# The last 64 rows: token weight, q tails and batch 1's k, v loaded in another shape and order, and the start planned anew

## The chip, the cores and the metric

The kernel runs on one core of one Trainium2 chip. The metric is the device time of one execution in microseconds. Three runs of the kernel before took 355.86, 356.5 and 356.73 us, median 356.5. One more execution was profiled; it took 356.91 us, and the span from its first to its last instruction is 355.1 us.

## The reference: what is computed

Linear attention, without a softmax, then an RMS norm per head, and a residual MLP that mixes tokens first and channels second. All inputs and the output are float32.

```python
kv  = einsum('bhsd,bhse->bhde', k, v)          # 8 batches, 8 heads, 576 rows, 64 channels
out = einsum('bhsd,bhde->bhse', q, kv)
x   = out / sqrt(mean(out*out, -1) + 1e-6) * g_norm      # heads side by side: [8, 576, 512]
tok = einsum('ts,bsd->btd', w_tok, alpha1*x + beta1)     # w_tok 576 x 576
u   = x + lam*tok
ch  = maximum((alpha2*u + beta2) @ w_ch1, 0) @ w_ch2     # 512 -> 2048 -> 512
y   = u + lam*ch
```

## The kernel before

**Tiling.** 576 rows are four chunks of 128 and a tail of 64. Chunk c of a tile holds every fourth row, since the loads give each partition four consecutive rows of 512 (`(p c) d`, c = 4); the last 64 rows, the tail, are loaded apart, on 64 partitions. Tails of an even and an odd batch share one tile of 128 partitions (`xtl`), so the MLP treats five chunks in odd batches and four in even ones. k and v have a second layout, "rows of nine" (`nine`): 64 partitions take nine consecutive rows each of one head, the other 64 partitions the same of its neighbour, 2304 bytes in one piece; the sum over rows in k'v does not care for their order.

**Stages of a batch.** k'v per head (`kv_product` on rows of nine, L695, or `kv_groups.main` and `tails` on rows of four, L798 and L808), split into two bf16 parts (`kvd`); q split likewise (`split_q`), turned (`qt_dma`: batch 1 on TensorE, L673, later batches by DMA transposes); the product q (k'v) and the norm (`qkv_groups`); the token product with the turned `w_tok` (`wt`) and the residual sum (`tok_groups`, `tok_first` for batch 0, L1242, sum at L1259); the turn of u (`ut_groups`; for batch 0 on TensorE, L1277); the channel MLP (`ch1_groups`, L1343 to L1370; `ch2_groups`, L1419). Batch 0 has its own fp32 code for the front: `kv_first`, `qt_first` (L730, and its tails L745) and `qkv_first` (L929, tails L954; the tail rows are scaled and rounded into `rtt` at L974 and L982).

**Constant work at the start.** `wt_groups` turns `w_tok`: its first 512 rows in L1565, its last 64 rows (`wst2`, 64 partitions of 576) by five TensorE transposes in L1588, and sums its columns in L1610 (`sums`, columns 0 to 511 and 512 to 575), which carries beta1 through the product. The staging tiles `wst`, `wst2` lie in `ht`, so that the MLP's first write of `ht` waits for their readers.

**What sets the order.** Every operation is noted with its engine, an assumed cost, what it reads and writes (keys). A list scheduler (`Prog.schedule`) then writes one static order per engine. Priorities follow from due times of the MLP's products (`mark`), and a table (`P.plan(due, 8, moves, on)`) adds to the priorities of single operations by their number, or fixes their engine. Until the first MLP product, where the scheduler sees nothing ready for TensorE, it writes filler products on a zeroed tile into the stream (`warm`, L1750); they stay in the stream whatever the real times are. The scheduler also assumes that TensorE's code comes in blocks of 256 instructions that take 5 to 6.6 us each (`fetched`, `fetch`).

**Loads.** All large loads go out on SyncE's queue in a fixed chain: for each half of batch 0's heads k, v, q and two q-tail loads (`load_first`, `load_q`, `load_first_tail`, L594); `w_tok` in two parts and its tail (L1521, L1525); then, behind a "gate" (the first four of nine products of batch 0's second half), batch 1's k and v (L608, with two tail loads each, L613) with `w_ch1`'s first quarter, q and the q tail between (L575), the other quarters (L1648), `lam`, and `w_ch2`'s quarters (L1659).

Of the kernel before, what the change touches and what calls it, by code (L numbers as in the profile page):

```python
# [19 lines left out]
TP = 640  # L20
# [443 lines left out]
def bass_transnormer_attn__then__resmlp_affine_kernel(  # L464
# [15 lines left out]
    with ExitStack() as stack:  # L480
# [38 lines left out]
        a2t = sb("a2t", [128, 4, TP + 16], BF16)  # L519
# [7 lines left out]
        wst2 = hst[0:64, 2304:2880]  # L527
# [39 lines left out]
        def load_main(tile, key, src, b, hs, eng="SP"):  # L567
# [4 lines left out]
                dma_us=3.7 if hs == ALL[0] else 1.5 if hs.start else 2.0)  # L572
# [11 lines left out]
        def load_first(a):  # L584
            for key, src, tile in (("kf", k, kf), ("vf", v, vf)):
                P.op("SP", 0.6, lambda e, src=src, tile=tile: e.dma_start(
                    nine(tile, 0, a).rearrange("p x c d -> p x (c d)"),
                    src[0, 4 * a:4 * a + 4].rearrange("(x y) (p c) d -> (y p) x (c d)",
                                                      y=2, c=9)),
                    w=[(key, a)], dma_us=2.0 if a and key == "vf" else 1.4)  # L590

        def load_first_tail(a):
            for y in range(2):
                P.op("SP", 0.45, lambda e, y=y: e.dma_start(  # L594
                    qft[0:64, 4 * a + 2 * y:4 * a + 2 * y + 2, :],
                    q[0, 4 * a + y:4 * a + y + 3:2, 512:576, :].rearrange("h s d -> s h d")),
                    w=[("qft0", a, y)], dma_us=0.2)

        def load_kv(b):
            j = (b + 1) % 2  # L600
            for tile, src, n in ((kf, k, "kf"), (vf, v, "vf")):
                if b > 1:
                    P.op("SP", 0.6, lambda e, src=src, tile=tile: e.dma_start(
                        tile[:, j].rearrange("p (z f) -> p z f", z=4),
                        src[b].rearrange("(z y) (p c) d -> (y p) z (c d)", y=2, c=9)),
                        w=[(n, j)], dma_us=3.1)
                    continue
                P.op("SP", 0.6, lambda e, tile=tile, src=src: e.dma_start(  # L608
                    rows512(tile).rearrange("p h c d -> p h (c d)"),
                    src[b, :, 0:512, :].rearrange("h (p c) d -> p h (c d)", c=4)),  # L610
                    r=["gate"], w=[(n, j)], dma_us=3.2)
                for g in range(2):
                    P.op("SP", 0.5, lambda e, tile=tile, src=src, g=g: e.dma_start(  # L613
                        rows64(tile)[64 * g:64 * g + 64],
                        src[b, 4 * g:4 * g + 4, 512:576, :].rearrange("h s d -> s h d")),
                        w=[(n + "t", g)], dma_us=0.2)

        def load_q(b, hs=ALL[0], tails=True):
            load_main(qf, "qf", q, b, hs)
            if tails:  # L620
# [8 lines left out]
        def split_q(b):  # L629
# [4 lines left out]
            for cs, hs in parts:  # L634
# [4 lines left out]
                if n == 1:  # L639
# [5 lines left out]
                kh, kl = ([qkeys(b, c, i, a) for c in cs for a in aa] for i in range(2))  # L645
# [7 lines left out]
        def qt_dma(b):  # L653
# [10 lines left out]
            for a, hs in enumerate(HALVES):  # L664
                for cs in PAIRS:
# [3 lines left out]
                    def f(e, cs=cs, t=t, hs=hs, n=n):  # L669
                        for h in range(4):  # L670
                            for i, c in enumerate(cs):
# [6 lines left out]
                                                           for x in keys_of(c, (a,))], w=[t])  # L678
                    P.op(act_dve(512 * n, 1.5), 0, lambda e, cs=cs, t=t, hs=hs, n=n: copy(
# [40 lines left out]
        def qt_first():  # L720
# [18 lines left out]
            def tail(a):  # L739
                t = P.ptile(1)  # L740

                def f(e):
                    for pr in range(2):
                        h = 4 * a + 2 * pr
# [36 lines left out]
        def kv_groups(b):  # L781
            if b > 1:
                yield from kv_nine(b)
                return
# [373 lines left out]
        def wtk(sc):  # L1158
            return [("wtm", sc)] if sc < 4 else [("wts", lo) for lo in (0, 512)]

        def tok_groups(b):
# [26 lines left out]
            def tails():  # L1188
                t = P.ptile(1)

                def f(e):
                    for sc in range(5):
                        for i in range(2):
                            w, r = tok_w(sc, 4), rsrc(i, sc)
                            if b >= MIX and sc == 4:
# [6 lines left out]
                                      for kk in wtk(s) + rkeys(i, s)], w=[t])  # L1202
# [313 lines left out]
        for i, hs in enumerate(HALVES):  # L1516
            load_first(i)
            load_q(0, hs, False)
            load_first_tail(i)
        for i in range(2):  # L1520
            P.op("SP", 0.6, lambda e, i=i: e.dma_start(  # L1521
# [271 lines left out]
```

## Time and profile before

| what | value |
|---|---|
| runs, median | 356.5 us |
| profiled execution, its own time | 356.91 us |
| its span | 355.1 us |
| TensorE busy | 344.1 us, 97% |
| VectorE, ScalarE, GpSimd busy | 238.7, 157.0, 22.2 us |
| DMA | 60.83 MB, mean 171 GB/s |
| granted TensorE clock | 1.00 throughout |
| first MLP product (L1343) | 31.09 us from the span's start |

How to read it: PE is TensorE's products, PEld its weight loads, DVE VectorE, ACT ScalarE, POOL GpSimd, SP SyncE, which issues loads and stores. A row of a timeline gives start, length, engine, line, operation, tiles, how many, and in brackets how long the engine idled before it and what ended that. A row of the chain of waits gives start, length and the work on the chain. A row of a window gives the busy time of each engine in that stretch, with the number of instructions.

### The profile page before, as it was taken

The numbers are of one execution on the slowest core, as the hardware profiler recorded it, in microseconds if no ns is written. First come the engines' busy times: TensorE is split into PE (matmuls) and PEld (weight loads), VectorE is DVE, ScalarE is ACT, GpSimd is POOL, SyncE is SP. The second block draws the span as 40 slices with busy tenths as digits, with TensorE's granted clock in tenths as the row PEclk, the third lists the DMA queues.
The fourth block names the chain that finished last, engine by engine and source line by source line (L and its number), as shares of the span: only waits on it lengthen the run. The fifth ranks groups of instructions, "written<-read, shape, count | busy, mean of one in ns | idle before, by whom it ended". The sixth has DMA issues, their size and how long they took to land.

```text
span 355.1 us, 7785 instructions
## 1 busy us (share of the span) xinstructions
PE 344.1 (97%) x3501; PEld 198.9 (56%) x3320; DVE 238.7 (67%) x365; ACT 157.0 (44%) x267; POOL 22.2 (6%) x30
## 2 busy tenths in 40 slices
PE   7998999999999999999999999999999999999996
PEld 6776644567554554467644654457744554457643
DVE  3679997874889579968883389945974378830021
ACT  3646961248722585038720386018620285007600
POOL 4161123300000000000000000000000000000000
PEclk9999999999999999999999999999999999999999
DMA  8999999999983599269704496244404010150022
GB/s 280 337 360 372 394 346 362 252 203 248 294 231 78 152 379 154 64 198 346 136 18 133 157 319 133 46 148 64 89 4 146 33 30 2 30 153 11 0 61 89
DMA packets 82761, 60.83 MB, mean 171 GB/s; under 512 B 55773, under 2 KB 66277, under 8 KB 82728
## 3 DMA queue, kind: packets, MB, share of 16 engines
q1 hardware_dynamic: 82704, 60.32, 58.7%
q8 instruction: 27, 0.44, 0.6%
q14 instruction: 6, 0.05, 0.0%
q10 hardware_dynamic: 24, 0.01, 0.0%
HBM read 38.82 MB, written 9.44 MB: 136 GB/s over the span
## 4 chain that ended last, share of the span: by engine, by line
PE 88%; DVE 6%; DMA 3%; issue 1%; SPq 0%
PE ps L1419 30%; PE ps L1370 18%; PE ps L1328 14%; PE ps L1168 7%; PE ps L695 4%; PE ps L1019 2%; PE ps L458 2%; PE ps L1197 1%; DMA vf<-in_v_dram 1%; DVE xm L1429 1%; DMA qt<-qs 1%; DVE a2b L1185 1%; DVE xm L1181 1%; PE ps L1400 1%; PE ps L1217 1%
## 5 line engine op out<-in xcount | busy, mean ns | idle before, releaser
L1419 PE MATMUL ps<-w,ht 128*128 128x512 bf16 x537 | 122.5, 379 | 2.3 <-issue 1.4
L1317 ACT ACTIVATE ht<-ps,hb 128x640 bf16<-128x640 f32 (+1 forms) x112 | 83.7, 747 | 48.7 <-PE ps L1370 35.9
L1419 PEld LDWEIGHTS ps<-w,ht 128*128 128x128 bf16 x560 | 53.5, 98 | 63.6 <-issue 2.0
L1370 PE MATMUL ps<-a2t,w 128*128 128x320 bf16 (+1 forms) x512 | 72.2, 299 | 0.4 <-DMA a2t<-a2b 0.4
L1370 PEld LDWEIGHTS ps<-a2t,w 128*128 128x128 bf16 x512 | 49.5, 98 | 21.4 <-DMA a2t<-a2b 0.8
L1328 PE MATMUL ps<-a2t,w 128*128 128x512 bf16 x232 | 52.7, 379 | 1.3 <-issue 0.6
L766 ACT ACTIVATE kvd<-ps 64x128 bf16<-64x128 f32 x24 | 6.5, 271 | 85.4 <-PE ps L695 85.3
L1328 PEld LDWEIGHTS ps<-a2t,w 128*128 128x128 bf16 x240 | 22.6, 98 | 26.5 <-DMA a2t<-a2b 0.4
L1429 DVE TENSOR_TENSOR xm<-ps,xm 128x512 f32<-128x512 f32 x31 | 20.7, 688 | 24.8 <-PE ps L1419 24.5
L1168 PE MATMUL ps<-rt,wt 128*128 128x512 bf16 x106 | 25.2, 379 | 0.4 <-issue 0.2
L1041 DVE TENSOR_REDUCE small<-sq 128x16 f32<-128x1024 f32 x14 | 16.8, 1214 | 12.9 <-ACT sq L1039 12.7
L1181 DVE TENSOR_TENSOR xm<-ps,xm 128x1024 f32<-128x1024 f32 x14 | 17.1, 1222 | 8.0 <-PE ps L1217 5.1
L695 PEld LDWEIGHTS ps<-vf,kf 64*64 64x64 f32 x1008 | 16.0, 135 | 6.3 <-issue 4.5
L564 ACT ACTIVATE qs<-qf 128x1024 bf16<-128x1024 f32 x13 | 13.4, 1049 | 13.5 <-DMA qf<-in_q_dram 10.7
L1185 DVE TENSOR_TENSOR a2b<-xm,a_bc 128x512 bf16<-128x512 f32 x28 | 18.7, 709 | 0.5
L771 DVE TENSOR_TENSOR kvd<-ps,kvd 64x128 bf16<-64x128 f32 x24 | 6.9, 288 | 18.0 <-ACT kvd L766 17.6
L695 PE MATMUL ps<-vf,kf 64*64 64x64 f32 x1008 | 17.9, 221 | 0.6 <-DMA vf<-in_v_dram 0.6
L1168 PEld LDWEIGHTS ps<-rt,wt 128*128 128x128 bf16 x112 | 10.9, 98 | 12.9 <-issue 0.4
L650 DVE TENSOR_TENSOR qs<-qf,qs 128x1024 bf16<-128x1024 f32 x14 | 16.9, 1217 | 1.5 <-ACT qs L564 1.5
L1060 DVE TENSOR_TENSOR xm<-ps,small 128x1024 f32<-128x1024 f32 x14 | 17.1, 1221 | 0.4
L1429 DVE TENSOR_TENSOR xtl<-ps,xtl 128x512 f32<-128x512 f32 x4 | 2.8, 692 | 20.2 <-PE ps L1419 20.1
L1019 PEld LDWEIGHTS ps<-kvd,qt 128*128 128x128 bf16 x224 | 13.9, 98 | 2.5 <-DMA qt<-qs 0.6
(146 smaller groups left out, 327.9 us busy)
## 6 DMA issues: line engine op xcount, KB each, us to landing
out_dram<-xm SPq DMA_DIRECT2D x31, 256.0 KB, 2.5
qf<-in_q_dram SPq DMA_DIRECT2D x7, 1024.0 KB, 11.4
kf<-in_k_dram SPq DMA_DIRECT2D x6, 1152.0 KB, 7.4
vf<-in_v_dram SPq DMA_DIRECT2D x6, 1152.0 KB, 8.5
stg<-in_moe_w_ch_dram SPq DMA_DIRECT2D x3, 1024.0 KB, 14.1
kf<-in_moe_w_ch_dram SPq DMA_DIRECT2D x2, 1024.0 KB
kf<-in_k_dram SPq DMA_DIRECT2D x2, 576.0 KB, 4.8
vf<-in_v_dram SPq DMA_DIRECT2D x2, 576.0 KB, 5.6
```

Of the source, the lines that this page charges most:

```text
L650: lambda e, hi=hi, lo=lo, src=src: e.tensor_tensor(out=lo, in0=src, in1=hi, op=ALU.subtract), r=kin + kh, w=kl, port=True)
L695: m = e.matmul(t.ap(slice(64 * x, 64 * x + 64))[:, y, 0:64], nine(kf, b, a)[r, x, c, :], nine(vf, b, a)[r, x, c, :], start=(c == 0), stop= ...
L1019: e.matmul(o, w, kvd[:, h, 0, :], start=True, stop=False)
L1060: P.op("DVE", dve_us(64 * m), lambda e: e.tensor_tensor(out=x3, in0=split(raw()), in1=inv, op=ALU.mult), r=[t, ("sm", sms)], w=xk, pri=-200)
L1168: m = e.matmul(t.ap()[:, i, :], tok_w(sc, c), rsrc(b, sc), start=(sc == 0), stop=(sc == 4))
L1181: P.op("DVE", dve_us(512 * n), lambda e: e.tensor_tensor(out=x, in0=t.ap(rows) if n > 1 else t.flat(rows), in1=x, op=ALU.add), r=[t] + xk, ...
L1185: P.op("DVE", dve_sb(512), lambda e, c=c: e.tensor_tensor(out=a2b[rows, c, :], in0=xv(b, (c,)), in1=a2_bc[rows, :], op=ALU.mult), r=xkeys( ...
L1317: o = P.op("ACT", act_us(n) + 0.07 * (b > 0), lambda e: e.activation(dst, src(), ACT.Relu, bias=hb[:, fj:fj + 1]) if b else e.activation(d ...
L1328: m = e.matmul(t.flat(), w, a2t[:, dj, 0:512], start=(dj == 0), stop=(dj == 3))
L1370: m = e.matmul(t.ap()[:, i, 0:n], w1[:, dj, 128 * fj:128 * fj + 128], a2t[:, dj, 320 * i:320 * i + n], start=(dj == 0), stop=(dj == 3))
L1419: m = e.matmul(t.flat(), ht[:, fj, 128 * c:128 * c + 128], w2[:, fj, :], start=(fj == 0), stop=(fj == 15))
L1429: P.op("DVE", dve_us(512), lambda e: e.tensor_tensor(out=x, in0=t.flat(), in1=x, op=ALU.add), r=[t] + keys, w=keys)
```

## The change

Six edits and a new table of moves.

1. The last 64 rows of `w_tok` go to 128 partitions: partition 2t + h holds half h of row t (256 values); the last 64 columns go to a small tile of their own, `wst3`. They are no longer turned by transposes, but by fp32 products with every second column of the identity, which pick out the rows of one half.
2. The turned tail gets keys of its own (`wtt`), so that products on token columns 0 to 511 no longer wait for it, nor for the second part of the column sums.
3. Batch 0's q tails are loaded by two transfers (even heads, odd heads) in place of four, behind `w_tok`'s first 512 rows; k, v, q of both halves move up.
4. Batch 1's k and v are loaded in rows of nine, two transfers in place of six, and go through `kv_nine`.
5. Batch 1's q tail goes to 128 partitions (heads 0 to 3 on the lower, 4 to 7 on the upper 64, four heads side by side), by two transfers; its split works on 128 x 256 values in place of 64 x 512, and one group of four transposes turns it, where there were two. It overwrites batch 0's q tail, whose readers it waits for.
6. `a2t` is wider by 48 columns, which nothing reads.
7. The table of moves has other entries: 69 operations with a changed priority where there were 46, and nine with a fixed engine where there were five. All operation numbers shift, so the entries do not compare one by one.

```diff
-        wst2 = hst[0:64, 2304:2880]
+        wst2, wst3 = hst[:, 2304:2560], hst[0:64, 2560:2624]
...
-        def load_first_tail(a):
-            for y in range(2):
-                P.op("SP", 0.45, lambda e, y=y: e.dma_start(
-                    qft[0:64, 4 * a + 2 * y:4 * a + 2 * y + 2, :],
-                    q[0, 4 * a + y:4 * a + y + 3:2, 512:576, :].rearrange("h s d -> s h d")),
-                    w=[("qft0", a, y)], dma_us=0.2)
+        def load_first_tail(y):
+            P.op("SP", 0.45, lambda e: e.dma_start(
+                qft[0:64, 4 * y:4 * y + 4, :], q[0, y:8:2, 512:576, :].rearrange("h s d -> s h d")),
+                w=[("qft0", a, y) for a in range(2)], dma_us=0.36)
...
         def load_kv(b):
             j = (b + 1) % 2
             for tile, src, n in ((kf, k, "kf"), (vf, v, "vf")):
-                if b > 1:
-                    P.op("SP", 0.6, lambda e, src=src, tile=tile: e.dma_start(
...
-                P.op("SP", 0.6, lambda e, tile=tile, src=src: e.dma_start(
-                    rows512(tile).rearrange("p h c d -> p h (c d)"),
-                    src[b, :, 0:512, :].rearrange("h (p c) d -> p h (c d)", c=4)),
-                    r=["gate"], w=[(n, j)], dma_us=3.2)
-                for g in range(2):
-                    P.op("SP", 0.5, lambda e, tile=tile, src=src, g=g: e.dma_start(
-                        rows64(tile)[64 * g:64 * g + 64],
-                        src[b, 4 * g:4 * g + 4, 512:576, :].rearrange("h s d -> s h d")),
-                        w=[(n + "t", g)], dma_us=0.2)
+                P.op("SP", 0.6, lambda e, src=src, tile=tile: e.dma_start(
+                    tile[:, j].rearrange("p (z f) -> p z f", z=4),
+                    src[b].rearrange("(z y) (p c) d -> (y p) z (c d)", y=2, c=9)),
+                    r=["gate"] if b == 1 else [], w=[(n, j)], dma_us=3.1)
 
         def load_q(b, hs=ALL[0], tails=True):
             load_main(qf, "qf", q, b, hs)
-            if tails:
+            if b == 1:
+                for g in range(2):
+                    P.op("SP", 0.6, lambda e, g=g: e.dma_start(
+                        qft[64 * g:64 * g + 64, 0:4, :],
+                        q[1, 4 * g:4 * g + 4, 512:576, :].rearrange("h s d -> s h d")),
+                        w=["qft1", "qft0"] + [("qft0", a, y) for a in range(2) for y in range(2)]
+                        if g == 0 else ["qft1g"], dma_us=0.35)
+            elif tails:
                 load_tail(qft, "qft%d" % (b % 2), q, b, 64 * (b % 2))
...
-                if n == 1:
+                if n == 1 and b == 1:
+                    src, hi, lo = qft[:, 0:4], qs[:, 4, 0:4, 0, :], qs[:, 4, 0:4, 1, :]
+                    kin, nh = ["qft1", "qft1g", "qft0"], 4
+                elif n == 1:
...
-                for cs in PAIRS:
+                for cs in PAIRS if a == 0 else PAIRS[:2]:
...
+                    if n == 1:
+                        P.op(act_dve(512, 1.5), 0, lambda e, t=t: copy(
+                            e, qt[:, :, 576:640].rearrange("p (g h) s -> p g h s", g=2),
+                            t.flat().bitcast(BF16)[:, 0:512].rearrange(
+                                "p (h g s) -> p g h s", h=4, g=2)),
+                            r=[t], w=[("qt", 4, x) for x in range(2)])
+                        continue
...
         def kv_groups(b):
-            if b > 1:
-                yield from kv_nine(b)
-                return
+            yield from kv_nine(b)
+            return
...
-        def wtk(sc):
-            return [("wtm", sc)] if sc < 4 else [("wts", lo) for lo in (0, 512)]
+        def wtk(sc, lo=0):
+            return [("wtt" if lo else "wtm", sc)] if sc < 4 else [("wts", lo)]
...
+        for what, i in (('k', 0), ('v', 0), ('q', 0), ('k', 1), ('v', 1), ('q', 1), ('w', 0), ('w', 1), ('t', 0), ('t', 1), ('w', 2)):
+            if what == "w":
+                load_wtok(i)
+            elif what == "q":
+                load_q(0, HALVES[i], False)
+            elif what == "t":
+                load_first_tail(i)
+            else:
+                load_first(i, what)
...
+                        for h in range(2 if sc < 4 else 1):
+                            r = slice(64 * h, 64 * h + 64)
+                            m = e.matmul(tail.flat(r)[:, 64 * sc:64 * sc + 64],
+                                         wst2[:, OFF[sc]:256:4] if sc < 4 else wst3,
+                                         ident[:, h:128:2] if sc < 4 else ident[r, r],
+                                         start=True, stop=True,
+                                         skip_group_check=True)
...
+        def load_wtok(i):
+            if i == 2:
+                P.op("SP", 0.6, lambda e: e.dma_start(
+                    wst2, moe_w_tok[512:576, 0:512].rearrange("t (h s) -> t h s", h=2)),
+                     w=["wst2"], dma_us=0.4)
+                P.op("SP", 0.6, lambda e: e.dma_start(wst3, moe_w_tok[512:576, 512:576]),
+                     w=["wst3"], dma_us=0.1)
```

More of the change, by code (lines that the diff above doesn't have):

```diff
@@ L644, in split_q @@
                     kin = [("qf", a) for a in aa]
-                kh, kl = ([qkeys(b, c, i, a) for c in cs for a in aa] for i in range(2))
+                kh, kl = ([qkeys(z, c, i, a) for c in cs for a in aa
+                           for z in ((0, 1) if c == 4 and b == 1 else (b,))] for i in range(2))
                 m = 64 * n * nh
@@ L1515, in bass_transnormer_attn__then__resmlp_affine_kernel @@
         P.chain = True
[L1516 to L1521, printed above, removed]
+        def load_wtok(i):
[5 more added lines that the diff above has]
+                     w=["wst3"], dma_us=0.1)
+                return
+            P.op("SP", 0.6, lambda e: e.dma_start(
                 wst[:, 2 * i:2 * i + 2, :],
@@ L1754, in bass_transnormer_attn__then__resmlp_affine_kernel @@
         P.plan(due, 8, {
[7 rows of a table removed]
-            154: "DVE", 181: "DVE", 182: "POOL", 211: "POOL", 215: "DVE"})
[10 rows of a table added]
+            59: "DVE", 67: "DVE", 88: "POOL", 148: "DVE", 177: "ACT", 180: "ACT", 182: "ACT",
+            184: "DVE", 204: "POOL"})
         P.synchronize()
```

39 lines of the change are left out of this document (15 added, 24 removed), and 17 rows, old and new, of the table start.

## The prediction

> **What bounds the kernel now.** I read the page first, from its top to the chain of waits.
>
> ```profile
> span 355.1 us, 7785 instructions
> PE 344.1 (97%) x3501; PEld 198.9 (56%) x3320; DVE 238.7 (67%) x365; ACT 157.0 (44%) x267; POOL 22.2 (6%) x30
> ...
> q8 instruction: 27, 0.44, 0.6%
> ```
>
> TensorE is busy 97% of the span, so a gain has to come out of TensorE time that computes nothing, or out of TensorE work itself. The next view is busy time by stretch: up to the first product of the channel MLP (31.09), up to the steady MLP (40.77), and on; the last columns are the granted clock, the busy share of the sixteen DMA engines, and GB/s.
>
> ```profile
> 5.89:31.09 25.20, 24.39 (x485) 19.35 (x490) 18.00 (x43) 14.85 (x38) 8.54 (x11) 1.00 1.06 350
> 31.09:40.77 9.68, 8.71 (x126) 6.40 (x96) 9.32 (x16) 7.11 (x10) 1.16 (x1) 1.00 1.03 394
> 40.77:60.00 19.23, 19.02 (x105) 8.50 (x107) 18.79 (x23) 10.29 (x20) 3.65 (x3) 1.00 1.04 371
> 66.00:81.00 15.00, 14.07 (x240) 9.12 (x224) 11.53 (x23) 5.40 (x12) 0.45 (x1) 1.00 0.95 181
> ```
>
> From 40.77 TensorE has no slack (19.02 of 19.23). From 31 to 60 VectorE is full too (28.11 of 28.91), and DMA throughout (1.06 to 1.03 to 1.04). The slack is before 40.77. I take it from the chain of waits, in order of time (start, length, what):
>
> ```profile
> 11.52 0.23 PE ps L954 x8
> ...
> 11.91 1.03 PE ps L1750 x4
> 12.94 1.21 PE ps L695 x72
> ...
> 15.31 0.33 PE ps L745 x2
> 15.65 0.54 PE ps L1750 x2
> ...
> 18.34 0.68 PE ps L1588 x5
> ...
> 23.63 0.25 PE ps L1610 x5
> ...
> 24.42 0.43 PE ps L1750 x2
> 24.86 0.44 PE ps L1242 x4
> 25.29 2.02 PE ps L798 x64
> 27.31 0.39 PE ps L808 x16
> ```
>
> L1750 are filler products on a zeroed tile, which the planner puts where it expects TensorE to wait: 1.03 + 0.54 + 0.43 = 2.00 us here. Two real stalls follow, in the timeline's brackets:
>
> ```profile
> 32.98 1.09 PE L1277 MATMUL ps<-ident,xm 128*128 128x128 f32 x8 [0.22 <-DVE xm L1259]
> 34.72 0.45 PE L673 MATMUL ps<-identb,qs 128*128 128x128 bf16 x5 [0.64 <-DVE qs L650]
> ```
>
> So **2.9 us** can be had before 40.77: 2.00 of filler and 0.86 of stalls. After it, 66 to 81 holds 15.00 - 14.07 = 0.9 more.
>
> **The change, part by part.** The sum runs against the profiled execution, 356.91 us with a span of 355.1, so 1.8 lie outside the span; the median of the runs, 356.5, is 0.4 below it.
>
> *TensorE work.* Three edits alter it. (a) Batch 1's q tails now lie on 128 partitions, four heads per half, so one group of four transposes falls away.
>
> ```profile
> 39.34 0.45 PE ps L673 x8
> ```
>
> These eight are the two tail groups; four cost half, **-0.22**. (b) Turning the token weight's last 64 rows: five transposes (0.68) become eight products of 128x64 and one of 64x64. The page counts two instructions per fp32 product, and the nearest rows are L798 (2.02 / 64 = 32 ns each) and L808 (0.39 / 16 = 24 ns): 16 x 0.032 + 2 x 0.024 = 0.55, **-0.13**. (c) Batch 1's k, v in rows of nine run the code that batches 2 to 7 use:
>
> ```profile
> 152.35 1.21 PE ps L695 x72
> 153.56 0.16 issue
> ```
>
> Twice 1.37 = 2.74 against 2.02 + 0.39 = 2.41: **+0.33**. Together -0.02: TensorE's work stays as it is. The 48 columns added to `a2t` shift addresses only; I cost them at nothing.
>
> [...]
>
> *Loads.* The timeline gives the issues on SP's queue (start, time that the issue held the queue), and the view of transfers, asked at each of them, the KB and the us from issue to landing, in the same order.
>
> ```profile
> 3.71 0.60 SPq L586 DMA_DIRECT2D kf<-in_k_dram  x1
> 4.35 0.47 SPq L586 DMA_DIRECT2D vf<-in_v_dram  x1
> 7.95 0.49 SPq L1525 DMA_DIRECT2D ht<-in_moe_w_tok_dram  x1
> 14.04 0.61 SPq L613 DMA_DIRECT2D kf<-in_k_dram  x1
> 19.62 0.75 SPq L613 DMA_DIRECT2D vf<-in_v_dram  x1
> ```
>
> ```profile
> kf<-in_k_dram SPq DMA_DIRECT2D x1, 576.0 KB, 5.8
> vf<-in_v_dram SPq DMA_DIRECT2D x1, 576.0 KB, 6.6
> ht<-in_moe_w_tok_dram SPq DMA_DIRECT2D x1, 144.0 KB, 10.0
> kf<-in_k_dram SPq DMA_DIRECT2D x1, 64.0 KB, 7.2
> vf<-in_v_dram SPq DMA_DIRECT2D x1, 64.0 KB, 5.2
> ```
>
> Batch 0's second v lands at 10.95, 1.4 us after its k (9.5), for 576 KB in rows of nine: 2.9 us per whole tensor. Batch 1's v, main part and tails, ends at 24.8, 3.6 us after k's tail at 21.2, for the same 1152 KB in the old form. So rows of nine save 0.7 each, **1.4 us** of a full DMA, and everything behind batch 1's v (w1's and w2's quarters) comes that much earlier. On SP's queue batch 0 issues two q-tail transfers where it had four, k, v of batch 1 two where they had six; the token weight's last rows two for one and batch 1's q tail two for one: four issues fewer of about 0.6 us. I cost that at nothing: SP runs 5 us ahead of the data (the last row: issued 19.62, landed 24.8), and this lead hides it both ways. Without the lead it would be worth 2.4.
>
> The last token rows "by sixteen engines" I also cost at nothing: DMA share is 1.06 in that stretch, so the engines are full whichever of them carry it. Bounds: 0 to the whole load, 144 KB at that stretch's 350 GB/s, 0.4 us. [...] No row here counts engines per transfer.
>
> One wait is added: batch 1's q tail overwrites batch 0's, so its load waits for L745, and behind it on SP queue w1's second to fourth quarters and the scale loads. L745 can run from about 17.5 (below), SP comes to it at 21 or sooner, and the lead of 5 us covers a wait of that size.
>
> *Order.* Batch 0's q tails move behind the token weight's main part. Half of them (64 KB) leave the queue ahead of the second k, v, q and all (128 KB) ahead of the token weight. At 350 GB/s that is 0.2 and 0.4 us, a lower bound, since these rows are the smallest, 256 bytes; I take twice that, 0.4 and 0.8. L745 and L954 must wait for what used to land with the token weight's last rows at 17.95, less their 0.4: about 17.5. The turned token rows (L1588) and the sum of their columns (L1610's 0.25) are no longer asked for by the first token product. These 0.93 us move behind the first MLP product but do not vanish.
>
> *What filler and stalls go.* (1) The filler at 11.91 lies between batch 0's first half and the second k, v, which had landed at 10.95, 2.0 us before L695 used them (12.94). What held it is not in the row; the candidates are the planner's own estimate and the loading of TensorE's code. v now lands at 10.55 and L745, L954 are out of the way. Bounds: 0, or all 1.03; I take half, **-0.5**. (2) The filler at 15.65 bridges to the token weight, which comes 0.8 earlier: all of it, **-0.5**. (3) The filler at 24.42 precedes the half-token products that wait for the tail row; half, **-0.2** of 0 to 0.43. (4) The stalls of 0.86 stem from VectorE; a row of the chain and two of the timeline:
>
> ```profile
> 28.76 0.81 DVE a2t L1287
> ```
>
> ```profile
> 29.79 0.94 DVE L830 TENSOR_TENSOR kvd<-ps,kvd 64x128 bf16<-64x128 f32 x3
> 30.76 0.93 DVE L833 COPY kvd<-kvd 64x256 bf16<-64x256 bf16 x4
> ```
>
> Batch 1's k-v splits stand between L1287 and the sum L1259 that L1277 waits for. They cost the same in rows of nine, but can be done 1.4 us sooner; one copy and half of a cast of the q tails go as well, uncosted. Half, **-0.4** of 0 to 0.86. After 40.77 nothing is sure: 0, within -0.9 and +0.9.
>
> Sum: 0.0 - 0.5 - 0.5 - 0.2 - 0.4 = -1.6. 356.9 - 1.6 = 355.3 as profiled, **354.9** as a median (span 353.5). About 0.3%, 1.1 us, is what a measurement of this kernel can tell from no change.
>
> **Rivals.** *A, hidden anyway.* VectorE (28.11 of 28.91 from 31 to 60) sets the pace, and what is taken out of the fillers returns as waits on its casts and scalings. For: its share. Against: TensorE never waits between 40.77 and 60 although VectorE is full. Time: only (2) stays, 356.5 - 0.5 = 356.0.
>
> *B, slower: the q tails come too late.* The tail rows of batch 0 pass L745, a copy, L954, a square, a reduction, a root, two scalings and L982 before the last fifth of the first token product, L1242 at 24.86.
>
> ```profile
> 17.29 0.41 DVE L982 TENSOR_TENSOR rtt<-xtl,e1g_bc 64x256 bf16<-64x256 f32 x1
> 19.91 0.59 DVE L974 TENSOR_TENSOR xtl<-ps,small 64x128 f32<-64x128 f32 x2
> 20.54 0.66 DVE L982 TENSOR_TENSOR rtt<-xtl,e1g_bc 64x256 bf16<-64x256 f32 x1
> ```
>
> ```profile
> 20.00:25.00 5.00, 4.84 (x94) 3.51 (x88) 4.05 (x9) 2.85 (x7) 2.37 (x5) 1.00 1.08 356
> ```
>
> The second tail took from 15.31 to 21.20, 5.9 us. From 17.5 that ends at 23.4, and the first tail, which used to be done at 17.70, brings VectorE work of the same kind, at least 1.25 us (0.59 + 0.66), into a stretch where 0.95 of 5 is free. Both then end near 24.9. It decides if the tail rows come later than the product would otherwise reach them, 24.86 less the 1.2 of (1) to (3), 23.7: 1.2 late, which eats these terms, and as much again if half 1's chain on VectorE, L1259 and the MLP's start are pushed back with it, against (4)'s 0.4. Time 356.5 + 1.2 - 0.4 = 357.3.
>
> *C, slower: TensorE's code.* 27 code loads for 6821 instructions of PE and PEld, if all are TensorE's, are 253 each. From 5.89 to 31.09 run 975, one per 26 ns. Rows of nine are 288 where L798 and L808 are 160: 128 more, 3.3 us if code loading is the pace and they stay ahead of the MLP. Against: from 31 on the stream is thin, and the new order may put them there. Time if half of it holds: 356.5 - 1.6 + 1.6, no change; in full 358.2.
>
> *D, all of it.* Fillers and stalls all go: 2.9, and some of 0.9: 356.5 - 3.3 = 353.2.
>
> **How the numbers follow.** Forecast 0.46, A 0.20, B 0.13, C 0.09, D 0.12. The forecast's unsure terms, (1) 0.5, (3) 0.2, (4) 0.4 either way and 0.9 after 40.77, spread it by about 1 us, so that three quarters of it (0.35) are below 355.4; with D and 0.04 of A, faster is 0.51. Same takes 0.10 of the forecast, 0.15 of A, 0.05 of C and 0.02 of B: 0.32. Slower is the rest, 0.11 of B, 0.04 of C and 0.02 of both others: 0.17. The range, 353.1 to 357.4, leaves out half of D below it and the far ends of B and C above.
>
> **What would show it.** Right: the first MLP product (31.09 before) near 29.5; L1750 after 5.89 down from nine to about four; the products that follow L1588 at about 0.55 us and behind that first product; batch 1's v landed near 23.4; the two L673 and L1277 stalls halved. B shows as a wait of the first token product on the tail rows' chain, C as issue gaps ahead of L695 without a transfer that is late, A as new waits on VectorE between 31 and 66. The forecast is wrong if the first MLP product is not earlier, or if it is and the last stretch from there to the end has grown by as much.

## The result and the profile after

The changed kernel takes 360.1 us (median of four runs, 359.4 to 361.7); the kernel before took 356.6 beside it on the same chip. The ratio is 1.0109, 95% interval 1.0070 to 1.0147: the change makes the kernel slower by 3.5 us, where 354.9 was forecast. The profiled execution took 359.63 us (span 357.8) against 356.91 (355.1), so the traces show 2.7 of the 3.5.

The page of the changed kernel, its first lines and the line of queue q8:

```profile
span 357.8 us, 7971 instructions
PE 349.0 (98%) x3615; PEld 199.5 (56%) x3391; DVE 235.6 (66%) x364; ACT 156.3 (44%) x264; POOL 27.0 (8%) x33
...
q8 instruction: 27, 0.44, 0.5%
```

The same stretches as before (length; busy time and count of PE, PEld, DVE, ACT and POOL; clock, DMA share, GB/s):

```profile
5.89:31.09 25.20, 25.00 (x557) 19.41 (x558) 15.90 (x39) 14.95 (x38) 10.37 (x12) 1.00 1.05 382
31.09:40.77 9.68, 8.04 (x94) 5.59 (x76) 7.47 (x13) 7.39 (x11) 3.56 (x3) 1.00 1.05 403
...
66.00:81.00 15.00, 15.00 (x220) 9.31 (x218) 12.09 (x25) 4.52 (x10) 0.00 (x0) 1.00 0.78 180
```

The start is denser than before and 66 to 81 is full now (14.07 of 15.00 before), yet 31 to 41 holds only 8.04 of TensorE. The chain of waits of the changed kernel says why (start, length, what):

```profile
6.09 1.28 PE ps L702 x72
...
9.95 1.29 PE ps L1769 x6
...
12.49 0.54 PE ps L1769 x2
...
16.80 0.21 PE ps L1769
...
21.39 1.36 PE ps L1606 x18
22.75 0.32 PE ps L1769
...
26.41 2.26 PE ps L702 x144
28.66 1.02 PE ps L1283 x8
29.69 1.53 PE ps L1248 x14
31.21 1.40 issue
32.61 0.83 PE ps L1248 x6
```

"issue" is time in which TensorE waited for nothing that the profile shows. The first product of the channel MLP comes at 33.26 (31.09 before), 2.17 us later: 0.20 because the first data came later (6.09 for 5.89), 1.40 for this pause, and 0.68 for turning the token weight's last rows, 1.36 (L1606) where the transposes took 0.68. The turning, and with it the sum of these columns (0.25 at 24.80), still stands ahead of that product; the prediction had both behind it. The rest is about even; the fillers, 1.29 + 0.54 + 0.21 + 0.32 = 2.36, are what they were: 1.03 + 0.54 + 0.43, and this row ahead of them in the chain of the kernel before, 2.38.

```profile
10.05 0.38 PE ps L1750
```

By 165 us all of that is won back: the waits of 0.3 to 0.6 us that the kernel before had up to 131 are gone, and the same pair of MLP products starts at 165.79 where it started at 165.74. What is lost for good comes later. The timelines of the kernel before and of the changed kernel, each with this pair and the first products of L1419 (now L1425) behind 168:

```profile
165.74 0.43 PE L1370 MATMUL ps<-a2t,w 128*128 128x320 bf16 x2
...
171.70 1.03 PE L1419 MATMUL ps<-w,ht 128*128 128x512 bf16 x4
```

```profile
165.79 0.43 PE L1376 MATMUL ps<-a2t,w 128*128 128x320 bf16 x2
...
172.62 1.03 PE L1425 MATMUL ps<-w,ht 128*128 128x512 bf16 x4
```

From +0.05 to +0.92 us: the chain shows what lies between.

```profile
159.39 7.58 DMA qft<-in_q_dram
166.98 0.02 issue
167.00 0.02 ACT qs L564
167.02 0.61 issue
167.64 0.81 ACT ht L1323
168.44 0.05 issue
168.49 1.26 PE ps L1376 x8
```

Batch 5's last rows of q go out behind the 1 MB of that batch's q and land at 166.98. ScalarE's split of them (L564) waits, the relu (L1323) stands behind it, and TensorE behind the relu. Then at 201:

```profile
196.13 1.21 PE ps L702 x72
197.34 1.83 PE ps L1425 x8
199.17 1.21 PE ps L702 x72
200.38 0.54 PE ps L1425 x2
200.92 1.55 issue
202.47 0.61 PE ps L1425 x2
```

This pause of 1.55 us is like that at 31.21, and nothing after it is won back.

Both pauses end 1.27 to 1.35 us after a packet of queue q8 has landed, the queue of instruction loads: 30.28 to 31.34, and 200.13 to 201.12 (start and end of the packet). For the second, the view of transfers between 200.1 and 201.2:

```profile
q1 hardware_dynamic: 221, 0.18, 50.4%
q8 instruction: 1, 0.02, 5.6%
```

27 such loads of 16 KB serve 3615 + 3391 records of TensorE's products and weight loads, 259 for each load, near the 256 that the planner takes for a block. At two of the 27 a pause shows.

A count in the trace of the changed kernel agrees with such blocks. With the waits that stand in TensorE's stream, 1217 records lie ahead of the first pause and 4545 ahead of the second. They are 3328 apart, 13 x 256, and the loads at the two pauses are the 4th and the 17th, 13 apart: 256 records for each, so both pauses fit a border of one division into blocks of 256. The 256 records ahead of each pause begin at 26.91 and 196.46, within the dense fp32 products of k and v, where one product takes 2.26 us / 144 = 16 ns: 210 and 236 of the 256 are such products and their weight loads. They had run out after 4.3 and 4.5 us; the next record ran 5.70 and 6.01 us after the first of them.

### The profile page after: what moved, and what is told of

Read it like the earlier page. It is cut to its first block, busy times and chain, and to the rows that moved or that the text cites. A ratio compares the mean times of both kernels' runs of the same rounds, so it can differ in the third digit from the quotient of the medians.

```text
span 357.8 us, 7971 instructions
## 1 busy us (share of the span) xinstructions
PE 349.0 (98%) x3615; PEld 199.5 (56%) x3391; DVE 235.6 (66%) x364; ACT 156.3 (44%) x264; POOL 27.0 (8%) x33
## 4 chain that ended last, share of the span: by engine, by line
PE 92%; DMA 3%; issue 1%; DVE 1%; SPq 1%; ACT 0%
PE ps L1425 34%; PE ps L1376 17%; PE ps L1334 15%; PE ps L1174 7%; PE ps L702 5%; DMA qft<-in_q_dram 2%; PE ps L1025 2%; PE ps L458 2%; PE ps L1203 1%; DMA vf<-in_v_dram 1%; PE ps L1248 1%; PE ps L1406 1%; PE ps L1223 1%; PE ps L1582 1%; PE ps L1769 1%
## 5 line engine op out<-in xcount | busy, mean ns | idle before, releaser
L1425 PE MATMUL ps<-w,ht 128*128 128x512 bf16 x560 | 125.8, 379 | 1.6 <-issue 1.6
L1323 ACT ACTIVATE ht<-ps,hb 128x640 bf16<-128x640 f32 (+1 forms) x112 | 83.7, 748 | 65.9 <-PE ps L1376 33.1
L1425 PEld LDWEIGHTS ps<-w,ht 128*128 128x128 bf16 x560 | 53.4, 98 | 66.1 <-issue 4.4
L1334 PE MATMUL ps<-a2t,w 128*128 128x512 bf16 x240 | 54.3, 379 | 0.0
L773 ACT ACTIVATE kvd<-ps 64x128 bf16<-64x128 f32 x28 | 7.6, 272 | 86.5 <-PE ps L702 86.3
L1174 PE MATMUL ps<-rt,wt 128*128 128x512 bf16 x112 | 26.0, 379 | 0.0
L702 PEld LDWEIGHTS ps<-vf,kf 64*64 64x64 f32 x1152 | 18.2, 135 | 6.6 <-issue 5.0
L702 PE MATMUL ps<-vf,kf 64*64 64x64 f32 x1152 | 20.2, 221 | 0.8 <-DMA vf<-in_v_dram 0.8
L778 DVE TENSOR_TENSOR kvd<-ps,kvd 64x128 bf16<-64x128 f32 x28 | 8.1, 288 | 18.0 <-ACT kvd L773 17.6
L564 ACT ACTIVATE qs<-qf 128x1024 bf16<-128x1024 f32 x14 | 14.3, 1048 | 8.5 <-DMA qf<-in_q_dram 8.5
L650 DVE TENSOR_TENSOR qs<-qf,qs 128x1024 bf16<-128x1024 f32 x13 | 15.6, 1218 | 0.4 <-ACT qs L564 0.3
```

The costliest lines, as they stand in the source:

```text
L702: m = e.matmul(t.ap(slice(64 * x, 64 * x + 64))[:, y, 0:64], nine(kf, b, a)[r, x, c, :], nine(vf, b, a)[r, x, c, :], start=(c == 0), stop= ...
L1174: m = e.matmul(t.ap()[:, i, :], tok_w(sc, c), rsrc(b, sc), start=(sc == 0), stop=(sc == 4))
L1323: o = P.op("ACT", act_us(n) + 0.07 * (b > 0), lambda e: e.activation(dst, src(), ACT.Relu, bias=hb[:, fj:fj + 1]) if b else e.activation(d ...
L1334: m = e.matmul(t.flat(), w, a2t[:, dj, 0:512], start=(dj == 0), stop=(dj == 3))
L1425: m = e.matmul(t.flat(), ht[:, fj, 128 * c:128 * c + 128], w2[:, fj, :], start=(fj == 0), stop=(fj == 15))
```

## The experiments

Every kernel was run beside the kernel before (medians 356.4, 356.3, 356.4 and 356.1 us in four groups), and each ratio is taken within its group.

**Moving the border of the blocks, late.** The edit puts satisfied waits into TensorE's stream, ahead of each group of products of the second MLP half in batches 2 and 3, so that the blocks behind them begin elsewhere in the work.

```diff
+                for _ in range(self.extra.get(o.idx, 0)):
+                    eng.wait_ge(sems["DVE"], 1)
                 ins = o.fn(eng)
...
+                if b in (2, 3):
+                    P.extra[o.idx] = 4
```

> Edit on the changed kernel: four waits on a semaphore that has long been reached stand ahead of each group of four products of the second MLP half in batches 2 and 3 (36 groups, about 104 instructions more by batch 4's k'v products); the order of all work is as in the changed kernel. Theory, code: the pause of 1.55 us ahead of an MLP product at 202.47 us, with a code load from 200.13 to 201.12 in it, is TensorE waiting for its own code, because a block of 256 instructions began inside batch 5's dense k'v products; with about 104 instructions more the block begins elsewhere in the sequence, where the kernel before has it, and the pause goes: 1.7 us faster than the changed kernel, less 0 to 0.5 for the waits; the wait of 0.70 at 168.49 stays. Rival, data: the pause is a wait for data that the trace doesn't name (the zeroed order of loads); it stays, and the time is that of the changed kernel or up to 0.5 more.

Measured: 361.7 us (359.8 to 363.9), ratio 1.0148, interval 1.0094 to 1.0201. The pause near 202 is gone, but the total is no better. The view of TensorE's waits in that execution (362.79 us) shows what came in its place, and that the pause at 32.7, ahead of the edit, is still there:

```profile
PE ps L1028 <- DMA qt<-qs: 2.3, 1, 2.3
PE ps L1251 <- issue: 1.5, 1, 1.5
```

The wait of 2.3 us, at 126, is for a transposing transfer of q that the new plan issues shortly before it is needed. Waits of this kind differ between the traces of kernels with the new plan: at the same place it is 1.0 us in the run below that leaves out part of batch 1's products, and none in the changed kernel.

The same in the kernel before, with five waits:

> The same edit on the kernel before, with five waits in place of four, so that the block of code begins at the same place in batch 5's k'v products (some 50 instructions after their start) as in the changed kernel. Theory, code: a pause of 1 to 2 us that the kernel before does not have appears just behind batch 5's second k'v products, near 200 us, with a code load in it: 1 to 2 us slower than the kernel before. Rival, data: nothing but the waits' own cost, 0 to 0.5 us slower.

Measured: 356.6 us, ratio 1.0015 (0.9986 to 1.0044), and no pause near 200. A miss: the shift alone does not bring a pause into the old plan. It also shows that the added waits by themselves cost nothing that can be measured.

**The late last rows of q.** The edit loads one batch's last rows of q ahead of its 1 MB of q.

```diff
+        TAIL[4].start = MAIN["qf", 4].start - 0.001
+        P.sequence.sort(key=lambda o: (o.start, o.idx))
         P.synchronize()
```

> Edit on the changed kernel: batch 4's q tail is issued just ahead of batch 4's q on SP in place of two issues behind it; nothing else moves. Theory: ScalarE's split of that tail is in front of a relu in ScalarE's order and waited for the load's landing at 166.98, and TensorE waited 0.70 us at 168.49 for the relu behind; the tail now lands by 163 and this wait goes: 0.9 us faster than the changed kernel. Rival: the wait at 168.49 comes from ScalarE's amount of work there, and 0.2 or less is won.

Measured: 360.8 us, ratio 1.0131 (1.0094 to 1.0169). The rows that were late are batch 5's; this moved batch 4's and so tested nothing. The wait at 169 (0.41 us) and the pause at 203 (1.56) stayed.

> Both edits on the changed kernel. Theory: the two late pauses are the whole of what the changed kernel loses, since its MLP products stood 0.05 us from those of the kernel before at 131 to 165 us: 2.6 us faster than the changed kernel, within 0.5 of the kernel before. Rival, the start: the new start costs time of its own that the profiled run did not show (the runs are 3.5 slower by their medians, the profiled ones 2.7), and 0.8 us or more is left against the kernel before.

Measured, with both edits: 360.0 us, ratio 1.0087 (1.0046 to 1.0127), with single runs from 357.7 to 362.3. Its profiled execution, the fastest, has no pause at 202 and keeps the one at 32.6 (1.54 us).

**The data ahead of the instruction load.** These runs ask whether the 1 MB of q on the same DMA engines holds the load back. First, batch 6's q goes out earlier in the changed kernel:

```diff
+        at = sp[sp.index(MAIN["qf", 6]) - 4].start
+        MAIN["qf", 6].start, TAIL[6].start = at - 0.002, at - 0.001
```

> The changed kernel with one edit: the loads of batch 6's q and of its last rows are issued four places earlier on SP, ahead of a store. Nothing else moves. Theory: the TensorE pause of 1.55 us near 202.5 is an instruction load (16 KB on queue q8, landed 201.12) that stood behind 1 MB of q data on the same DMA engines (issued 194.1, landed 201.2). With that data gone earlier the pause falls under 0.4 us, and the last product of the MLP comes about 1.5 us earlier than in the changed kernel (profile near 358.1). Rival, the place of the block of instructions alone: the pause stays at 1.5 and the time with it (359.6).

Measured: 359.7 us, ratio 1.0088 (1.0061 to 1.0115); the pause is 1.15 us, the load runs from 199.92 to 201.06. Neither theory's number. What stood around q before, a transposing transfer and the stores, now filled the same stretch (queue q1 takes 114.4% of the engines' time from 196 to 200), so the engines were not free. Then the reverse, in the kernel before, with its shift and batch 6's q and last rows ahead of k and v (the same two lines, with 2 for 4):

> The kernel before, with five satisfied waits ahead of each group of four products of batches 2 and 3 (the shift alone: no pause near 200, time unchanged), and batch 6's q and its last rows loaded two places earlier on SP, ahead of that batch's k and v. Theory, a block boundary in the dense products and 1 MB queued ahead of the instruction load are needed together: a pause of 1 to 2 us appears near 200 and stays to the end, about 358.0. Rival, something else of the new plan makes the pause: no pause, 356.5.

Measured: 356.5 us, ratio 1.0000 (0.9986 to 1.0015), no pause. A miss that tells nothing: in the old plan batch 6's loads lie near 160, and those near 200 are batch 7's. With batch 7's moved:

> The kernel before, with the satisfied waits that shift the blocks of instructions, and batch 7's q and its last rows loaded two places earlier on SP, ahead of that batch's k and v, so that about 1 MB is queued on the DMA engines when the block of instructions for the work behind batch 5's k and v is asked for (near 196). The earlier run with batch 6's loads moved those of 160 us and tested nothing at 200. Theory, the load of instructions stands behind that data: a pause of 1 to 2 us at 199 to 202, 358.0. Rival, data on the queues do not matter: no pause, 356.5.

Measured: 356.5 us, ratio 1.0019 (1.0000 to 1.0038), and again no pause that the view of waits lists. But the load moved. Without q on the queue (the run with the shift alone) it falls between 196.9 and 198.2, 2.3 us after batch 5's first products of k and v begin (timeline):

```profile
194.64 1.28 PE L698 MATMUL ps<-vf,kf 64*64 64x64 f32 x72
```

With q issued at 194.50 it starts at 199.68, 5.5 us after the same products:

```profile
194.16 1.28 PE L700 MATMUL ps<-vf,kf 64*64 64x64 f32 x72
```

So queued data delay the load by some 3 us. Here border and data came together, and still next to nothing was lost. The trace shows why: behind 4545 records, the count that lies ahead of the second pause in the changed kernel, two products are 0.14 us apart where these products follow each other every 0.03 us.

```profile
201.86 0.19 PE L461 MATMUL ps<-kvd,qt 128*128 128x64 bf16 x1
202.00 0.20 PE L1024 MATMUL ps<-kvd,qt 128*128 128x64 bf16 x1
```

The load landed at 200.70, 1.3 us earlier. So the pause is there, but 0.1 us long. The 256 records ahead of it begin at 195.09 and last 6.8 us and not 4.5, since only 164 of them are dense. The counter-test in the changed kernel loads batch 6's q behind batch 7's k and v, and leaves TensorE's instructions as they are:

```diff
+        at = sp[sp.index(MAIN["qf", 6]) + 4].start
+        late = {MAIN["qf", 6]: at + 0.001, TAIL[6]: at + 0.002}
...
+        for o, t0 in late.items():
+            o.start = t0
```

> The changed kernel; batch 6's q and its last rows are loaded behind batch 7's k and v on SP (issued near 201 and not at 194.1), and the splits of that q follow later. The instructions of TensorE and their order stay. Theory, the data on the DMA engines belong to the cause: with no q queued at 194 the block of instructions for the work behind batch 5's k and v starts at 196 to 197 (200.1 in the changed kernel) and the pause of 1.55 us near 202.5 is gone or under 0.3. Rival, the place of the block in the dense products alone: the load takes as long and the pause stays over 1.2. The q is late for its own batch, so the total says nothing here.

Measured: the load starts at 198.57, 1.76 us after the first of these products (4.00 in the changed kernel), and there is no pause. The chain of waits of that run:

```profile
196.81 1.21 PE ps L704 x72
198.02 1.83 PE ps L1427 x8
199.85 1.25 PE ps L704 x72
```

TensorE's next products (L1427) follow at 200.99 without a gap. Its total, 360.5 us in its one execution, says nothing here, since q is late for its own batch. The pause near 202 thus needs two things together: 256 instructions that run out early, and data ahead of the load. Its length is what the second takes beyond the first: in the changed kernel the 256 records ahead of it ran out after 4.46 us and the next one ran after 6.01, 1.55 later.

**The same cause at the start.** Batch 1's products of k and v run over five of their nine groups of rows; four ninths of these products are left out.

```diff
+            some = 5 if b == 1 else 9
...
-                (range(9), []),)
+                (range(some), []),)
```

> The changed kernel, but batch 1's products of k and v run over 5 of the 9 groups of rows (the output lacks the other four; the order of all instructions is kept). That takes 128 TensorE instructions, 1.07 us, out of the start. Theory of instruction loads: the pause of 1.4 us ahead of the first MLP product goes or shrinks under 0.5, and that product comes 2.0 to 2.6 us earlier (near 30.9); the blocks behind it shift by 128 instructions, so the pause near 202 goes too, and the end comes 3.5 to 4.5 us earlier (355 to 356). Rival, the first MLP product waits for data (the last rows of the token weight, q's last rows): it comes 1.07 us earlier at most, the later pauses stay, and the end is 358.5.

Measured: 358.2 us, ratio 1.0047 (1.0032 to 1.0063). Both pauses are gone. TensorE's timeline:

```profile
6.83 1.28 PE L702 MATMUL ps<-vf,kf 64*64 64x64 f32 x72 [1.12 <-DMA vf<-in_v_dram]
...
32.02 1.24 PE L1351 MATMUL ps<-a2t,w 128*128 128x512 bf16 x5
```

From the first product on data to the first MLP product are 25.19 us (33.26 - 6.09 = 27.17 in the changed kernel): 1.98 less, where the removed products account for about 1. The end came less early than expected (356 at most); its trace shows waits of 1.0 us for a transposing transfer of q and of 0.8 at 168.

This run changes work. The next changes none: it shifts every border by 42 instructions ahead of the first data.

```diff
+        fills = [o for o in P.sequence if P.warm[3] in o.tiles][:28]
+        for o in fills[:7]:
+            o.fn = lambda e: warm(e, P.warm[3], 512)
+        P.sequence = [o for o in P.sequence if o not in fills[7:]]
+        for o in P.sequence:
+            o.deps.difference_update(fills[7:])
```

> The changed kernel with 42 TensorE instructions fewer ahead of all others: of the 44 products of zeros that keep TensorE busy until the first data are there, 28 of 128 columns become 7 of 512. No other instruction is changed or moved. Every border of 256 instructions comes 21 products later in the work. Theory, TensorE waits for its instructions (a block of 256 is asked for as TensorE enters the block before it, and 256 instructions with batch 1's or batch 5's 144 products of k and v among them run in less time than the load takes): the pause of 1.40 us ahead of the first MLP product and that of 1.55 at 202.5 both fall under 0.4, and the last MLP product comes 2.5 to 3.0 us earlier than in the changed kernel; 357.0 us. Rival, the pauses come from data that arrive late: both stay, 359.6 to 360.

Measured: 357.7 us (357.5 to 358.3), ratio 1.0041 (1.0028 to 1.0054): 2.4 us off the loss, a little less than expected. The instruction load near 200 is as late as ever (200.40 to 201.34). But the record behind the border, counted as above, now runs at 202.84, 1.50 us after the landing and without a gap. Of the 2.1 us between the spans (355.7 and 357.8) 0.6 is there at 162 already (the same MLP product at 162.22 and 162.80), so most of the gain is the second pause. The view of TensorE's waits has no pause for instructions left:

```profile
PE ps L1376 <- ACT ht L1323: 0.8, 1, 0.8
PE ps L1376 <- DMA a2t<-a2b: 0.6, 1, 0.6
PE ps L673 <- DVE qs L650: 0.2, 1, 0.2
```

The first of these is the late split of q's last rows. With batch 5's rows moved this time (`TAIL[5]` ahead of `MAIN["qf", 5]`):

> The kernel of the run just ahead, and batch 5's last rows of q loaded ahead of the 1 MB of that batch's q (they landed at 166.98, and ScalarE's split of them held up the relu that TensorE waited for at 168.5). If that wait is the third part of the loss, 0.8 to 0.9 us more go: 356.1 us, not slower than the kernel before. Rival, the wait moves to the next load: as the run ahead, 357.

Measured: 357.0 us, ratio 1.0016 (1.0003 to 1.0029), span 355.2. That wait is gone, and the products that the changed kernel started at 172.62 start at 171.72:

```profile
171.72 1.03 PE L1427 MATMUL ps<-w,ht 128*128 128x512 bf16 x4
```

**The turning products.** They cost 1.36 us where 0.55 was forecast. Their identity columns have a stride, and so have their weights. The first run gives the identity neighbouring columns, so that the turned rows hold other values:

```diff
-                                         ident[:, h:128:2] if sc < 4 else ident[r, r],
+                                         ident[:, 64 * h:64 * h + 64] if sc < 4 else ident[r, r],
```

> The changed kernel, but the products that turn the token weight's last rows take 64 neighbouring columns of the identity and not every second one (so those turned rows hold other values). Theory, the moving operand's stride makes these fp32 products slow: the 18 of them take 0.55 to 0.75 us and not 1.36. Rival, it is the strided weights or the product form itself: they stay at 1.3 to 1.4.

Measured (one execution, as for the next run): no change; 1.43 us as the timeline shows the 18, as in the changed kernel. My theory fell. The second gives the weights neighbouring columns, again with other values in the turned rows:

```diff
-                                         wst2[:, OFF[sc]:256:4] if sc < 4 else wst3,
+                                         wst2[:, 64 * sc:64 * sc + 64] if sc < 4 else wst3,
```

> The changed kernel, but the products that turn the token weight's last rows read 64 neighbouring columns of them as weights and not every fourth (so these turned rows hold other values). Theory, the stride of 16 bytes makes each load of weights take 214 ns and not the 138 of the same shape without a stride, and the 18 of them set the pace: 1.36 us becomes 0.6 to 0.9. Rival, neither stride counts and the shape 128 x 64 with a change of column group is slow: it stays at 1.3.

Measured: 0.95 us for the 18 in the timeline. The groups by line and shape (busy time, mean ns of one weight load), first of the changed kernel and then of this run:

```profile
L1606 PEld LDWEIGHTS ps<-ident,ht 128*64 128x64 f32 x16 | 1.0, 214 | 0.2 <-DVE small L968 0.2
```

```profile
L1606 PEld LDWEIGHTS ps<-ident,ht 128*64 128x64 f32 x16 | 0.6, 136 | 0.2 <-DVE small L968 0.2
```

**All three repaired,** with nothing left out of the computation: 42 instructions fewer, batch 5's last rows of q early, and one copy on ScalarE that lays the rows out in the order in which the products read them.

```diff
+        wst2c = hst[:, 2624:2880]
...
-                                         wst2[:, OFF[sc]:256:4] if sc < 4 else wst3,
+                                         wst2c[:, 64 * OFF[sc]:64 * OFF[sc] + 64] if sc < 4 else wst3,
...
+        pack = P.op("ACT", 0.4, lambda e: copy(
+            e, wst2c.rearrange("p (c m) -> p c m", c=4),
+            wst2.rearrange("p (m c) -> p c m", c=4)), r=["wst2"], w=["wst2c"])
```

> The changed kernel with three repairs, nothing left out: 42 TensorE instructions fewer ahead of the data, batch 5's last rows of q ahead of that batch's q, and one copy of 128 x 256 on ScalarE (0.3 to 0.4 us, in an idle stretch of 0.53 us near 19.5) that puts the token weight's last rows in the order in which the turning products read them, so that their weights have no stride. If the strided weights cost 0.5 us on the path, the turning products take 0.9 and not 1.36 us and the whole 356.5 us, equal to the kernel before (356.4). Rival, that 0.5 us goes into a wait for the next tile: 357.0 as without the copy. If all of the change's own gain is still there, 355.5.

Measured: 356.1 us (355.5 to 356.5), ratio 0.9994 (0.9982 to 1.0006). The chain and the timeline of this run:

```profile
21.37 0.88 PE ps L1609 x18
```

```profile
31.20 1.89 PE L1352 MATMUL ps<-a2t,w 128*128 128x512 bf16 x8
```

The first MLP product is at 31.20 (31.09 before), the span 354.6 us (355.1 before). Step by step: 360.1 - 2.4 (borders) - 0.7 (q's last rows) - 0.9 (weights without a stride) = 356.1. These steps compare runs of different groups, in which the kernel before has medians from 356.6 down to 356.1. The last step is the least sure: the two traces differ by 0.6 (spans 355.2 and 354.6), of which the turning products show 0.48. The repaired change is even with the kernel before; no version here beats it.

## Why the prediction was wrong

*What bounds the kernel* held: TensorE is busy 97 to 98% of the span, and most of the loss was time in which it did not compute; the strided weights are the exception.

*Two steps of the sum failed.* The first is "After 40.77 nothing is sure: 0, within -0.9 and +0.9". I took it as noise around the old order; but the order of the whole kernel is new. The bound was used up between 66 and 81 alone (-0.9), and then came +0.9 at 168 and +1.55 at 201, which put the end where it is. The second is the gain of 1.6 before 40.77: the first MLP product was forecast near 29.5 and came at 33.26, and at 31.20 with all three repairs.

*Rival C, TensorE's code,* had the mechanism and the 128 additional instructions right, and 0.09 as its chance; the forecast's sum has no term for it. I looked for a price of the mean rate (one instruction per 26 ns) and only up to 31. What counts is the one block whose 256 instructions run faster than the next is loaded: 1.40 us at the start, ahead of L1248 and not L695, and the same again at 201 in products that the change does not touch. I argued against C that the stream is thin from 31 on, but at 196 it is as dense as at 26. Three runs show it: both pauses go with 42 instructions fewer (2.4 us off) and with 128 fewer in the dense products, and the second goes with q out of the load's way.

*(a)* was right: L673 has four transposes fewer. *(b), the turning,* was mis-sized: -0.13 forecast, +0.68 measured. I priced it by L798, whose weights lie side by side; the weights here are four floats apart, and one such load takes 214 ns and not 136. Without the stride the 18 took 0.88, still 0.2 more than the transposes: at the 32 ns of L798 the 16 larger ones would be an estimated 0.51 of it, and for the rest I had no term. *(c), rows of nine,* was +0.33 forecast; the 144 records take 2.26 us against 2.41 for L798 and L808, so -0.15. As TensorE time they are cheaper; through the border of a block, they cost.

*Loads* were right in direction. Batch 1's v lands at 22.57 (issued 14.15, and 8.4 to landing), against 24.8 before and 23.4 forecast. The view of transfers at its issue:

```profile
vf<-in_v_dram SPq DMA_DIRECT2D x1, 1152.0 KB, 8.4
```

The earlier data bought nothing at the start, since TensorE did not wait for v there. That rows of 256 bytes go slower, on which the doubling for the q tails rests, shows in the trace of the kernel before: a packet of 256 bytes takes 18 ns there and one of 1024 bytes 46 (medians), 1.6 times as long for each byte.

*Fillers, (1) to (3),* -1.2 in all: nothing of it came. Ten fillers in place of nine after the first data, 2.36 us in place of 2.38; the planner put them elsewhere. What it expects TensorE to wait for at 9.95 was not tested and stays open. *(4), the stalls of L1277 and L673,* went from 0.86 to 0.22, more than the 0.4 forecast.

*Rival A* (a full VectorE) does not explain the loss: no wait on VectorE over 0.25 us is left after 31 in the repaired run. *Rival B's* chain does end late (the tail rows' product runs at 32.83), but with the pause gone it runs 1.2 us earlier without a wait, so it was the pause that held it. *D* (fillers and stalls all go) did not come: the stalls went, the fillers stayed.

## What to carry to other kernels

Before moving instructions, count TensorE's instructions between the borders of its blocks (here 256 records for each load, 3328 for 13), and look where the densest products (here 16 ns each) would fall: a block of them with its load behind queued data cost 1.4 and 1.55 us here, once in a stage that the change does not touch. A change in the number of instructions early on reached a border 170 us later here: 42 fewer, of work that only keeps TensorE busy, removed both pauses, at 31 and at 201. Price an operation by a row with the same strides, not only the same shape (a load of weights of the same shape took 214 ns with a stride and 136 without). And where a plan is made anew, compare the two traces along their whole length by the start of the same product, since a gain in the stage that was changed can be lost in one that was not.

## What the hardware showed that I had not expected

An instruction load of 16 KB took 0.9 to 1.5 us in the changed kernel (1.05 and 0.99 at the pauses), but the next instruction started 1.27 and 1.35 us after it had landed (1.24 to 1.59 at the pauses of all runs). With data queued the load came later: it started 2.3 us after the dense products began with the queue free and 5.5 with 1 MB of q ahead (1.76 and 4.00 in the other pair of runs). The trace does not show when a block is asked for; that it is as TensorE enters the block before, as I had it for the run with 42 instructions fewer, was my assumption. At the two pauses the load starts 3.4 and 3.7 us after the counted start of the block before; for all 27 loads this lies between 4.4 us before and 4.1 after that start, so the count says when only roughly.

A load of fp32 weights of 128 x 64 took 214 ns with a stride of 16 bytes and 136 without; a stride of 8 bytes in the moving identity cost nothing that can be seen (the 18 take 1.43 us with it and without): with the stride of the weights gone and that of the identity kept, the median product takes 222 ns, as those of L798 with neither.
